# Asking for lam on another queue and taking its powers on GpSimd, in a linear-attention and gated feed-forward kernel

## The chip, the cores and the metric

The kernel runs on one core of a Trainium2 chip. The metric is device time in microseconds (us), the median of several executions: 204.59 us before the change, of three runs between 204.53 and 204.88. The profile is one execution of its own, with a span of 203.0 us. Engines are named PE (TensorE), ACT (ScalarE), DVE (VectorE), POOL (GpSimd) and SP (SyncE, which here only issues transfers).

## The reference, cut to what matters

Two stages follow each other: a linear attention with a decay per head, and a feed-forward layer whose gate is a cosine.

```python
# q, k, v: (4 batches, 8 heads, 768 positions, 64); lam: (8,), between 0.97 and 0.99
# attention, block by block of 64 positions:
intra = (q_b @ k_b.T * lam ** (i - j), lower triangle) @ v_b
inter = (q_b * lam ** (i + 1)) @ kv_state
out_b = intra + inter
kv_state = lam ** 64 * kv_state + (k_b * lam ** (63 - j)).T @ v_b
# feed-forward on x = attention output as (3072, 512):
h = x @ w_in            # 512 x 2048
result = (h * cos(h)) @ w_out   # 2048 x 512
```

Inputs and outputs are float32. Every decay in the formula is a power of lam with a position as exponent. A product of a power at the position of q and an inverse power at the position of k gives the same decay, and that is how the kernel uses it.

## The kernel before, in words

**Tiles.** The 3072 rows are cut into 24 blocks of 128 rows; one block holds all 8 heads. The feed-forward works on tiles of 2 or 4 blocks (`TILES`, L21). Each tile makes 16 slices of the hidden layer (`hidden`, L734, output `ps_h`), takes their cosine on ScalarE (`cosine`, L741), multiplies on VectorE (`gated`, L746), and multiplies with w_out (`project`, L779, output `ps_f`). Attention of the later blocks is worked in between.

**The spans.** The first four blocks are handled apart, as two spans of 256 rows (`add_span`, L584), so that the feed-forward can begin early. In a span each partition holds two neighbouring rows. The span's q and k come as float32 in loads of 512 KB on SyncE's queue (`add_span_load`, L274), in the order q, k of the first span, q, k of the second. `prep` (L597) multiplies them with `q_sp` and `k_sp`, powers of lam for two rows per partition; then they are turned on TensorE (L606), copied out by ScalarE (L609), and the scores, the state and the values follow. q and k of the first span and q of the second are scaled on VectorE, k of the second on GpSimd (`QK`, L32). The span's v comes through GpSimd's queue as bfloat16, unscaled, and is asked for only when the first q has landed.

**The other blocks.** `prepare` (L329) multiplies q with `q_scale` and v with `v_scale`, powers of lam for one row per partition and six blocks per batch.

**The powers, before.** They are made in the set-up, ahead of everything: lam is loaded to all 128 partitions (L187) as the first transfer on SyncE's queue, with 8 numbers per partition. ScalarE takes the logarithm (L215), VectorE multiplies with the positions (L217 and L222), and ScalarE takes four exponentials (L220 to L229), two of them with the sign turned. Logarithm, exponential and sine each need a table loaded on ScalarE, so there are three table loads (at L215, L220 and L231); the last is for the cosine. The positions are made by GpSimd's iota.

**What sets the order.** A planner in the kernel (`Planner`, L56) gives each task an engine, a duration and a priority, simulates the engines and writes the instructions out in the order of the simulated starts. `SETUP` (L61) says when each engine is done with the set-up. Between the planned tasks of TensorE `keep_awake` (L866) puts filler matmuls into `ps_idle`, as many as the plan has time for, until the main block of the first tile.

Of the kernel before, what the change touches and what calls it, by code (L numbers as in the profile page):

```python
# [10 lines left out]
F32 = mybir.dt.float32  # L11
BF16 = mybir.dt.bfloat16
AF = mybir.ActivationFunctionType
ALU = mybir.AluOpType
# [41 lines left out]
class Planner:  # L56


    LAT = {"PE": 0.2, "ACT": 0.06, "DVE": 0.08, "POOL": 0.1, "SP": 0.0, "DMA": 0.0, "SETUP": 0.0}

    SETUP = {"POOL": 3.7, "DVE": 5.6, "ACT": 7.3, "SP": 1.3, "DMA": 2.9}  # L61

    def __init__(self, bufs):
        self.tasks, self.bufs = [], bufs
# [6 lines left out]
    def order(self):  # L71
        free, done = dict(self.SETUP), []
        got = {tag: [] for tag in self.bufs}
# [70 lines left out]
def kernel(  # L144
# [10 lines left out]
    nc = tc.nc  # L155
    B, H, S, D = q.shape
    P = 128
    NB = S // P
# [9 lines left out]
    def where(n):  # L168

        if n < 2 * SPANS:  # L170
            return n // 2, n % 2
        g, c = divmod(n // 2, NB)
        return 2 * g + n % 2, c
# [3 lines left out]
    consts = ctx.enter_context(tc.tile_pool(name="consts", bufs=1))  # L177
# [5 lines left out]
    def bank(i, shape, dt, name):  # L183
        return psum.tile(shape, dt, tag=f"bank{i}", bufs=1, name=name)

    lam_bc = consts.tile([P, H], F32)
    nc.sync.dma_start(out=lam_bc, in_=bass.AP(tensor=lam.tensor, offset=lam.offset, ap=[[0, P], [1, H]]))  # L187
    pos = consts.tile([P, NB], F32)
    nc.gpsimd.iota(pos, pattern=[[P, NB]], base=-S // 2, channel_multiplier=1,
                   allow_small_or_imprecise_dtypes=True)  # L190
    ident = consts.tile([P, P], BF16)
    make_identity(nc, ident)
    pos_sp = consts.tile([P, 2], F32)
    nc.gpsimd.iota(pos_sp, pattern=[[1, 2]], base=-S // 2, channel_multiplier=2,
                   allow_small_or_imprecise_dtypes=True)
    mask_sp = consts.tile([P, 2, P], F32)
    nc.gpsimd.memset(mask_sp, 1.0)
    for i in range(2):
        m = mask_sp[i * D:(i + 1) * D].rearrange("u k (s t) -> u k s t", s=2)
        nc.gpsimd.affine_select(out=m, in_=m, compare_op=ALU.is_ge, fill=0.0,  # L200
                                base=0, pattern=[[-1, 2], [1, 2], [2, D]], channel_multiplier=-2)
    mask = consts.tile([P, D], F32)
    nc.gpsimd.memset(mask, 1.0)
    for i in range(2):
        m = mask[i * D:(i + 1) * D]
        nc.gpsimd.affine_select(out=m, in_=m, compare_op=ALU.is_ge, fill=0.0,
                                base=0, pattern=[[1, D]], channel_multiplier=-1)
# [3 lines left out]
    nc.vector.memset(blank, 0.0)  # L211
    kv_bd = consts.tile([P, 2, NP, P], BF16)
    nc.vector.memset(kv_bd, 0.0)
    lnl = consts.tile([P, H], F32)
    nc.scalar.activation(lnl, lam_bc, AF.Ln)  # L215
    expo_sp = consts.tile([P, H, 2], F32)
    nc.vector.tensor_mul(expo_sp, pos_sp.unsqueeze(1).to_broadcast([P, H, 2]),  # L217
                         lnl.unsqueeze(2).to_broadcast([P, H, 2]))
    q_sp = consts.tile([P, H, 2], F32)
    nc.scalar.activation(q_sp, expo_sp, AF.Exp)  # L220
    expo = consts.tile([P, NB, H], F32)
    nc.vector.tensor_mul(expo, pos.unsqueeze(2).to_broadcast([P, NB, H]),  # L222
                         lnl.unsqueeze(1).to_broadcast([P, NB, H]))
    k_sp = consts.tile([P, H, 2], F32)
    nc.scalar.activation(k_sp, expo_sp, AF.Exp, scale=-1.0)
    q_scale = consts.tile([P, NB, H], F32)
    nc.scalar.activation(q_scale, expo, AF.Exp)
    v_scale = consts.tile([P, NB, H], F32)
    nc.scalar.activation(v_scale, expo, AF.Exp, scale=-1.0)  # L229
    warm = consts.tile([P, 1], F32)  # L230
    nc.scalar.activation(warm, halfpi, AF.Sin)  # L231


    spare = consts.tile([P, 112], F32)
# [7 lines left out]
    pl = Planner({**BUFS, "q_f": BUFS["ld"], "k_f": BUFS["ld"], "v_f": BUFS["ld"]})  # L242
# [9 lines left out]
    def prio_attn(n, part):  # L252
        i = next(i for i in range(len(TILES)) if n < first[i + 1])
        return begins[i - 1] + unit[i - 1] * (n - n % 2 - first[i] + 2 * part) / TILES[i]

    load_t, issue_t = {}, {}
    last_issue = {}

    def dma(queue, us, issue_us, emit, prio, deps=(), get=None, ordered=True, lat=1.9):
        t = pl.add(queue, issue_us, list(deps) + [last_issue.get(queue) if ordered else None], emit, prio, get=get)  # L260
        if ordered:
            last_issue[queue] = t
        d = pl.add("DMA", us, [t], None, prio, lat=lat)
        d.issue = t
        return t, d
# [40 lines left out]
    w_t, pace = {}, []  # L306
# [15 lines left out]
    T, So, Vo, d_t, Uo, Uo_sp = ({} for _ in range(6))  # L322
    qkT_head, qk_head, v_head, v12 = {}, {}, {}, {}
# [5 lines left out]
    def prepare(pr):  # L329

        b, c = where(2 * pr)
        early = 2 * pr < TILES[0] + 2
        vec = {"DVE": nc.vector, "POOL": nc.gpsimd}
        us = {"DVE": 0.69, "POOL": 1.05}
        pa = lambda part: prio_attn(2 * pr, part)

        def new_qk():
            if ("qk", pr) not in live:
                live["qk", pr] = toks.tile([P, 2, H, 2, D], BF16, tag="qk", bufs=BUFS["qk"], name="qk")
            return live["qk", pr]  # L340

        def prep_q(_, s, e):
            vec[e].tensor_mul(new_qk()[:, 0, :, s], live.pop(("q_f", 2 * pr + s)),  # L343
                              q_scale[:, c, :].unsqueeze(2).to_broadcast([P, H, D]))

        def prep_k(_, s):
            (nc.scalar.copy if early else nc.gpsimd.tensor_copy)(new_qk()[:, 1, :, s], live.pop(("k_f", 2 * pr + s)))  # L347

        def prep_v(_, s, e):
            live["v_s", 2 * pr + s] = toks.tile([P, H, D], BF16, tag="v_s", bufs=BUFS["v_s"], name="v_s")  # L350
            vec[e].tensor_mul(live["v_s", 2 * pr + s], live.pop(("v_f", 2 * pr + s)),  # L351
                              v_scale[:, c, :].unsqueeze(2).to_broadcast([P, H, D]))

        a, k_ = [], []
        for s in range(2):
            n = 2 * pr + s
            eq = "DVE" if early and s == 0 else "POOL"
            ev = "DVE" if early and s == 1 else "POOL"
            a.append(pl.add(eq, us[eq], [load_t["q_f", n]] + a, partial(prep_q, s=s, e=eq), pa(-0.9), get=None if s else "qk"))
            k_.append(pl.add("ACT" if early else "POOL", 0.61, [load_t["k_f", n]] + ([] if early else [a[0]]), partial(prep_k, s=s), pa(-0.9)))  # L360
            d_t[n] = v_head[n] = pl.add(ev, us[ev], [load_t["v_f", n]], partial(prep_v, s=s, e=ev), pa(-0.85), get="v_s")
            for name, t in (("q_f", a[s]), ("k_f", k_[s]), ("v_f", d_t[n])):
                issue_t[name, n].frees = [t]

        def new_T():
            if ("qkT", pr) not in live:
                live["qkT", pr] = toks.tile([P, 2, H, P], BF16, tag="qkT", bufs=BUFS["qkT"], name="qkT")
            return live["qkT", pr]

        def transposes(t, i):  # L370
            live["t", pr, i] = bank(t.bank[0], [P, H, P], BF16, "ps_t")
            for h in range(H):
                nc.tensor.transpose(live["t", pr, i][:, h, :], live["qk", pr][:, i, h], ident)

        def transposes_out(_, i):
            nc.vector.tensor_copy(new_T()[:, i], live["t", pr, i])

        def transposes_dma(_, i):
            return nc.sync.dma_start_transpose(out=new_T()[:, i], in_=live["qk", pr][:, i].rearrange("t h s d -> t (h s d)"))

        for i, src in enumerate((a, k_)):
            get = None if i else "qkT"
            if 2 * pr >= DMA_FROM:
                head, T[pr, i] = dma("SP", 1.4, 1.3, partial(transposes_dma, i=i), 2 * pr + i - LAG + 1.5,
                                     src + ([qkT_head[pr]] if i else []), get=get, ordered=False)
                T[pr, i].lat = 1.2
                if i and 2 * pr + LAG < NBLK:
                    issue_t["q_f", 2 * pr + LAG].deps.append(head)
            else:
                t = pl.add("PE", MM(P, 8), src + ([T[pr, 0]] if i else []), partial(transposes, i=i), pa(-0.05 + 0.05 * i), banks=1)  # L390
                head = T[pr, i] = pl.add("DVE", 0.7, [t], partial(transposes_out, i=i), pa(0.0), get=get)
                t.bank_frees = [[head]]
            if i == 0:
                qkT_head[pr] = head
        qk_head[pr] = a[0]
# [76 lines left out]
    def add_stretch(pr):  # L472

        n0 = 2 * pr
        g, c = divmod(pr, NB)
        pa = lambda part: prio_attn(n0, part)
        tile_i, j0 = tile_of(n0)

# [343 lines left out]
    for at, name in enumerate(names):  # L822
        which, n = name[0], int(name[1:])
# [12 lines left out]
        else:  # L836
            kept.append(add_load(n, which + "_f", src[which], at, deps))

    idle = pl.add("SETUP", 0.0, [], None, -1e9, banks=1)
    for x in range(SPANS):  # L840
        add_span(x)
    add_span_state()
    for pr in range(SPANS, NBLK // 2):
        prepare(pr)
# [70 lines left out]
```

## Time and profile before

| | before |
|---|---|
| device time, median | 204.59 us |
| span of the profile | 203.0 us |
| busy: PE, DVE, ACT, POOL | 195.0, 116.7, 119.8, 64.5 us |
| PE busy on ps_h (L737) and on ps_f (L783) | 90.5, 88.3 us |
| lam: issue to landing | 3.0 us |
| the span's q and k (512 KB each): median issue to landing | 5.1 and 5.6 us |
| table loads in the set-up | 3 of 1.28 us |
| HBM traffic | 27.27 MB read, 6.29 MB written |

The page gives busy time by engine, then the span in 40 slices with a digit for the tenths that an engine was busy. The chain of waits is followed back from the last instruction, each step to what released it. A line of the timeline gives start, length, engine, line and operation, "output<-input" with the shapes, the count, and in brackets the idle time before it with what ended it; consecutive instructions of one kind are merged. The engine names with a q (SPq, POOLq) are the queues that issue transfers. A line of packets counts the pieces that the transfers moved in a stretch of time, and how many were below each size.

### The profile page before, as it was taken

How to read it: one execution, taken by the hardware profiler on the slowest of the kernel's cores; microseconds unless marked ns; L12 is line 12 of the kernel's file. 1: busy time of each engine (PE TensorE's matmuls, PEld its weight loads, DVE VectorE, ACT ScalarE, POOL GpSimd, SP SyncE). 2: the span in 40 equal slices, each digit the busy share in tenths (PEclk: the TensorE clock that was granted, in tenths of full speed). 3: DMA queues.
4: the chain of work that ended last, by engine and by line, in shares of the span. 5: the costliest groups of instructions: out<-in, count | busy, mean ns of one | idle time of the engine just before them, and what ended most of it. 6: DMA issues, size and time to landing. Idle time of an engine off the chain costs nothing.

```text
span 203.0 us, 5951 instructions
## 1 busy us (share of the span) xinstructions
PE 195.0 (96%) x2457; PEld 118.0 (58%) x2485; DVE 116.7 (57%) x229; ACT 119.8 (59%) x240; POOL 64.5 (32%) x85
## 2 busy tenths in 40 slices
PE   6999999999999999999999999999999999999993
PEld 2567444547747857767658676755446444444463
DVE  2887783257955967758458575835589544444001
ACT  5978871128838868565639666644887555354120
POOL 5794004066034262726455272543500000000000
PEclk9999999999999999999999999999999999999999
DMA  4999999989989999999999899979900010111112
GB/s 129 318 193 203 204 197 217 194 204 238 204 218 164 257 213 230 233 183 262 205 268 211 181 213 244 226 184 261 208 1 3 3 52 0 52 55 52 52 74 81
DMA packets 96906, 33.94 MB, mean 167 GB/s; under 512 B 84336, under 2 KB 93936, under 8 KB 96880
## 3 DMA queue, kind: packets, MB, share of 16 engines
q1 hardware_dynamic: 89376, 28.78, 64.8%
q0 software_dynamic: 7360, 4.72, 16.2%
q8 instruction: 19, 0.31, 0.6%
q10 hardware_dynamic: 144, 0.07, 0.1%
q14 instruction: 7, 0.06, 0.1%
HBM read 27.27 MB, written 6.29 MB: 165 GB/s over the span
## 4 chain that ended last, share of the span: by engine, by line
PE 84%; DMA 8%; SPq 2%; issue 2%; DVE 1%; POOL 1%; ACT 0%; POOLq 0%; ACTq 0%
PE ps_h L737 41%; PE ps_f L783 35%; DMA v_f<-in_v_dram 4%; DMA sp_f<-in_k_dram 3%; SPq L268 2%; DMA k_f<-in_k_dram 2%; PE ps_o L483 2%; PE ps_kv L433 2%; PE ps_o L515 2%; PE ps_s L421 1%; PE ps_o L643 1%; PE ps_kv L630 1%; POOL k_sp L598 1%; PE ps_x L483 0%; DVE v_s L351 0%
## 5 line engine op out<-in xcount | busy, mean ns | idle before, releaser
L749 DVE TENSOR_TENSOR g<-ps_h,cos 128x256 bf16<-128x256 f32 (+1 forms) x148 | 73.2, 503 | 42.9 <-ACT cos L743 42.0
L743 ACT ACTIVATE cos<-ps_h,halfpi 128x256 f32<-128x256 f32 (+1 forms) x148 | 75.6, 538 | 29.4 <-PE ps_h L737 28.6
L737 PE MATMUL ps_h<-xT,w_in_sb 128*128 128x256 bf16 (+1 forms) x586 | 90.5, 304 | 0.5 <-issue 0.3
L783 PE MATMUL ps_f<-w_out_sb,g 128*128 128x512 bf16 (+2 forms) x394 | 88.3, 362 | 2.0 <-issue 1.3
L737 PEld LDWEIGHTS <-w_in_sb 128*128 128x128 bf16 x592 | 57.1, 98 | 30.0 <-DVE xT L523 0.4
L783 PEld LDWEIGHTS <-g 128*128 128x128 bf16 x416 | 38.6, 98 | 36.3
L343 POOL TENSOR_TENSOR qk<-q_f,q_scale 128x512 bf16<-128x512 f32 x19 | 19.6, 1043 | 37.9 <-DMA q_f<-in_q_dram 33.6
L797 ACT COPY o_sb<-ps_f 128x512 f32<-128x512 f32 (+1 forms) x24 | 13.7, 572 | 30.3 <-PE ps_f L783 29.1
L351 POOL TENSOR_TENSOR v_s<-v_f,v_scale 128x512 bf16<-128x512 f32 x19 | 19.6, 1043 | 17.8 <-DMA v_f<-in_v_dram 14.4
L426 DVE TENSOR_TENSOR s_m<-ps_s,mask 128x512 bf16<-128x512 f32 x20 | 13.0, 684 | 3.6 <-PE ps_s L421 3.0
L347 POOL CAST qk<-k_f 128x512 bf16<-128x512 f32 x18 | 11.0, 611 | 7.0 <-DMA k_f<-in_k_dram 6.8
L523 ACT CAST xT<-ps_o 128x512 bf16<-128x512 f32 x11 | 6.0, 588 | 9.6 <-PE ps_o L515 6.3
L439 DVE TENSOR_TENSOR sum<-sum,ps_kv 128x512 f32<-128x512 f32 x15 | 10.2, 681 | 0.6
L444 ACT CAST S<-sum 128x512 bf16<-128x512 f32 x15 | 9.2, 617 | 0.9 <-DVE sum L439 0.8
L797 DVE COPY o_sb<-ps_f 128x256 f32<-128x256 f32 (+1 forms) x2 | 0.7, 358 | 11.2 <-PE ps_f L783 11.2
L875 PE MATMUL ps_idle<-blank 128*128 128x512 f32 (+2 forms) x8 | 5.4, 824 | 1.6 <-DVE blank L211 1.6
L483 PEld LDWEIGHTS <-v_s 64*64 64x64 bf16 x320 | 3.9, 107 | 4.1 <-issue 3.6
L622 DVE TENSOR_TENSOR s_m_sp<-ps_s,mask_sp 128x512 bf16<-128x512 f32 x8 | 5.1, 682 | 1.0 <-PE ps_s L617 1.0
L483 PE MATMUL ps_o<-s_m,v_s 64*64 64x64 bf16 x256 | 5.1, 196 | 0.1
L711 POOL CAST S<-sum 128x512 bf16<-128x512 f32 x1 | 0.6, 606 | 14.0 <-DVE sum L708 14.0
L500 DVE COPY spare<-ps_o 1x1 f32<-1x1 f32 x5 | 0.8, 156 | 7.3 <-PE ps_o L483 7.3
L515 PE MATMUL ps_o<-qkT,S 64*64 64x64 bf16 x304 | 4.8, 194 | 0.0
(74 smaller groups left out, 94.5 us busy)
## 6 DMA issues: line engine op xcount, KB each, us to landing
q_f<-in_q_dram SPq DMA_DIRECT2D x20, 256.0 KB, 3.8
k_f<-in_k_dram SPq DMA_DIRECT2D x20, 256.0 KB, 4.1
v_f<-in_v_dram SPq DMA_DIRECT2D x20, 256.0 KB, 4.7
out_dram<-o_sb SPq DMA_DIRECT2D x19, 256.0 KB, 2.6
w_out_sb<-in_moe_w_out_dram POOLq DMA_DIRECT2D x4, 512.0 KB, 12.6
out_dram<-o_sb SPq DMA_DIRECT2D x9, 128.0 KB, 3.4
sp_f<-in_q_dram SPq DMA_DIRECT2D x2, 512.0 KB, 5.1
sp_f<-in_k_dram SPq DMA_DIRECT2D x2, 512.0 KB, 5.6
```

Of the source, the lines that this page charges most:

```text
L343: vec[e].tensor_mul(new_qk()[:, 0, :, s], live.pop(("q_f", 2 * pr + s)), q_scale[:, c, :].unsqueeze(2).to_broadcast([P, H, D]))
L347: (nc.scalar.copy if early else nc.gpsimd.tensor_copy)(new_qk()[:, 1, :, s], live.pop(("k_f", 2 * pr + s)))
L351: vec[e].tensor_mul(live["v_s", 2 * pr + s], live.pop(("v_f", 2 * pr + s)), v_scale[:, c, :].unsqueeze(2).to_broadcast([P, H, D]))
L426: nc.vector.tensor_mul(t, live["s", pr][s], mask.unsqueeze(1).to_broadcast([P, H, D]))
L439: nc.vector.tensor_add(new, live["sum", pr, 0] if half else live["sum", pr - 1, 1], live["kv", pr][half])
L444: nc.scalar.copy(new_S(pr, half), live["sum", pr, half])
L483: yield lambda h=h: nc.tensor.matmul(o[halves[h % 2], h // 2], lhsT=live["v_s", n0 + s][m, h, :], rhs=live["s_m", n0 + s][m, h, :], start= ...
L737: nc.tensor.matmul(t[:, :n], lhsT=w_in_sb[:, kd, f * P:(f + 1) * P], rhs=live["xT", i][:, kd, at], start=(kd == 0), stop=(kd == KD - 1))
L743: nc.scalar.activation(c[:, :n], live["h", i, f, at.start][:, :n], AF.Sin, bias=halfpi)
L749: return nc.vector.tensor_mul(live["g", i][:, f, at], live.pop(("h", i, f, at.start))[:, :n], live.pop(("c", i, f, at.start))[:, :n])
L783: nc.tensor.matmul(live["f", i, j, piece][:, :width], lhsT=live["g", i][:, f, j * P:(j + 1) * P], rhs=w_out_sb[:, f, part], start=(f == 0) ...
L797: (nc.scalar.copy if eng == "ACT" else nc.vector.tensor_copy)(o[:, :width], live["f", i, j, piece][:, :width])
```

## The change

lam is asked for on ScalarE's queue, so that q stands first on SyncE's. The powers are no longer made by logarithm and exponential: GpSimd raises lam to the positions with its two-input power operation. For that the positions exist with both signs (four iotas instead of two). `scale_sp` (8 heads, two signs, two rows: 32 numbers per partition) is made at the end of GpSimd's set-up. `scale` (two signs, six blocks, 8 heads: 96 per partition) is a planned task `scales_t` of GpSimd, which stands after the issue of the third w_out piece; `prep_q` and `prep_v` of the other blocks depend on it. ScalarE keeps one table load, for the cosine. The numbers in `SETUP` are changed, which changes the sizes of a few fillers on TensorE: the first float32 run ends with 128 instead of 256 columns, one 512-column filler before the first scores is left out, and the one before the second span's k transposes has 512 instead of 320 columns. The other instructions keep their order on every engine.

```diff
-    SETUP = {"POOL": 3.7, "DVE": 5.6, "ACT": 7.3, "SP": 1.3, "DMA": 2.9}
+    SETUP = {"POOL": 4.0, "DVE": 4.5, "ACT": 2.6, "SP": 0.85, "DMA": 2.45}
...
-    nc.sync.dma_start(out=lam_bc, in_=bass.AP(tensor=lam.tensor, offset=lam.offset, ap=[[0, P], [1, H]]))
-    pos = consts.tile([P, NB], F32)
-    nc.gpsimd.iota(pos, pattern=[[P, NB]], base=-S // 2, channel_multiplier=1,
-                   allow_small_or_imprecise_dtypes=True)
+    nc.scalar.dma_start(out=lam_bc, in_=bass.AP(tensor=lam.tensor, offset=lam.offset, ap=[[0, P], [1, H]]))
+    pos = consts.tile([P, 2, NB], F32)
+    for i, sign in enumerate((1, -1)):
+        nc.gpsimd.iota(pos[:, i], pattern=[[sign * P, NB]], base=-sign * S // 2, channel_multiplier=sign,
+                       allow_small_or_imprecise_dtypes=True)
...
-    lnl = consts.tile([P, H], F32)
-    nc.scalar.activation(lnl, lam_bc, AF.Ln)
-    expo_sp = consts.tile([P, H, 2], F32)
-    nc.vector.tensor_mul(expo_sp, pos_sp.unsqueeze(1).to_broadcast([P, H, 2]),
-                         lnl.unsqueeze(2).to_broadcast([P, H, 2]))
-    q_sp = consts.tile([P, H, 2], F32)
-    nc.scalar.activation(q_sp, expo_sp, AF.Exp)
...
     warm = consts.tile([P, 1], F32)
     nc.scalar.activation(warm, halfpi, AF.Sin)
+
+    def power(out, p, lam_axis, pos_axis):
+        nc.gpsimd.tensor_tensor(out, lam_bc.unsqueeze(lam_axis).to_broadcast(list(out.shape)),
+                                p.unsqueeze(pos_axis).to_broadcast(list(out.shape)), op=ALU.pow)
...
+    scale_sp = consts.tile([P, H, 2, 2], F32)
+    power(scale_sp.rearrange("p h a s -> p h (a s)"), pos_sp.rearrange("p a s -> p (a s)"), 2, 1)
+    q_sp, k_sp = scale_sp[:, :, 0], scale_sp[:, :, 1]
+    scale = consts.tile([P, 2, NB, H], F32)
+    q_scale, v_scale = scale[:, 0], scale[:, 1]
...
+    def scales(_):
+        power(scale.rearrange("p a n h -> p (a n) h"), pos.rearrange("p a n -> p (a n)"), 1, 2)
+
+    scales_t = pl.add("POOL", 2.0, [], scales, -100.0)
...
-            a.append(pl.add(eq, us[eq], [load_t["q_f", n]] + a, partial(prep_q, s=s, e=eq), pa(-0.9), get=None if s else "qk"))
+            a.append(pl.add(eq, us[eq], [load_t["q_f", n], scales_t] + a, partial(prep_q, s=s, e=eq), pa(-0.9), get=None if s else "qk"))
...
+    scales_t.deps.append(w_t["out", 2].issue)
```

More of the change, by code (lines that the diff above doesn't have):

```diff
@@ L186 @@
     lam_bc = consts.tile([P, H], F32)
-    nc.sync.dma_start(out=lam_bc, in_=bass.AP(tensor=lam.tensor, offset=lam.offset, ap=[[0, P], [1, H]]))
-    pos = consts.tile([P, NB], F32)
-    nc.gpsimd.iota(pos, pattern=[[P, NB]], base=-S // 2, channel_multiplier=1,
-                   allow_small_or_imprecise_dtypes=True)
+    nc.scalar.dma_start(out=lam_bc, in_=bass.AP(tensor=lam.tensor, offset=lam.offset, ap=[[0, P], [1, H]]))
[3 more added lines that the diff above has]
+                       allow_small_or_imprecise_dtypes=True)
     ident = consts.tile([P, P], BF16)
     make_identity(nc, ident)
-    pos_sp = consts.tile([P, 2], F32)
-    nc.gpsimd.iota(pos_sp, pattern=[[1, 2]], base=-S // 2, channel_multiplier=2,
-                   allow_small_or_imprecise_dtypes=True)
+    pos_sp = consts.tile([P, 2, 2], F32)
+    for i, sign in enumerate((1, -1)):
+        nc.gpsimd.iota(pos_sp[:, i], pattern=[[sign, 2]], base=-sign * S // 2, channel_multiplier=2 * sign,
+                       allow_small_or_imprecise_dtypes=True)
     mask_sp = consts.tile([P, 2, P], F32)
@@ L213 @@
     nc.vector.memset(kv_bd, 0.0)
-    lnl = consts.tile([P, H], F32)
-    nc.scalar.activation(lnl, lam_bc, AF.Ln)
-    expo_sp = consts.tile([P, H, 2], F32)
-    nc.vector.tensor_mul(expo_sp, pos_sp.unsqueeze(1).to_broadcast([P, H, 2]),
-                         lnl.unsqueeze(2).to_broadcast([P, H, 2]))
-    q_sp = consts.tile([P, H, 2], F32)
[L220 to L229, printed above, removed]
     warm = consts.tile([P, 1], F32)
     nc.scalar.activation(warm, halfpi, AF.Sin)
+    def power(out, p, lam_axis, pos_axis):
[6 more added lines that the diff above has]
+    q_scale, v_scale = scale[:, 0], scale[:, 1]
     spare = consts.tile([P, 112], F32)
@@ L358, in prepare @@
             ev = "DVE" if early and s == 1 else "POOL"
-            a.append(pl.add(eq, us[eq], [load_t["q_f", n]] + a, partial(prep_q, s=s, e=eq), pa(-0.9), get=None if s else "qk"))
+            a.append(pl.add(eq, us[eq], [load_t["q_f", n], scales_t] + a, partial(prep_q, s=s, e=eq), pa(-0.9), get=None if s else "qk"))
             k_.append(pl.add("ACT" if early else "POOL", 0.61, [load_t["k_f", n]] + ([] if early else [a[0]]), partial(prep_k, s=s), pa(-0.9)))
-            d_t[n] = v_head[n] = pl.add(ev, us[ev], [load_t["v_f", n]], partial(prep_v, s=s, e=ev), pa(-0.85), get="v_s")
+            d_t[n] = v_head[n] = pl.add(ev, us[ev], [load_t["v_f", n], scales_t], partial(prep_v, s=s, e=ev), pa(-0.85), get="v_s")
             for name, t in (("q_f", a[s]), ("k_f", k_[s]), ("v_f", d_t[n])):
```

## The prediction

> **What bounds the kernel now.** I read the page first (engine shares and slices), then the stages, the chain of waits, and last the timeline and the transfers of the first microseconds, because the diff touches only work done there.
>
> From the page, the engine shares and the 40 slices:
>
> ```profile
> PE 195.0 (96%) x2457; PEld 118.0 (58%) x2485; DVE 116.7 (57%) x229; ACT 119.8 (59%) x240; POOL 64.5 (32%) x85
> PE   6999999999999999999999999999999999999993
> ```
>
> TensorE is full in all slices but the first and the last. The waits of TensorE from 15 us to the end add up to only 1.6 us (1.3 before the second product, 0.3 before the first). So the kernel is a start-up of about 11 us and then a solid block of matmuls; a change in the start-up is worth exactly what it moves the beginning of that block. The chain of waits says what sets the beginning (start us, length us, what):
>
> ```profile
> 0.81 0.40 SPq L187
> 1.26 0.42 SPq L268
> 1.73 0.58 SPq L268
> 2.35 1.54 SPq L268
> 3.93 5.95 DMA sp_f<-in_k_dram
> ...
> 10.06 1.05 POOL k_sp L598
> 11.16 0.40 PE ps_t L606 x4
> 11.55 0.55 PE ps_kv L630 x8
> ```
>
> The chain begins with the issue of lam (L187), goes through SyncE's queue and the fourth span load (the second k), then GpSimd's scaling of it, then TensorE, which never stops again. Busy TensorE before 11.16 us is filler (ps_idle). The other operations of that stage, from the timelines of ScalarE, VectorE and GpSimd (start us, length us):
>
> ```profile
> 3.79 0.21 ACT L215 ACTIVATE lnl<-lam_bc 128x8 f32<-128x8 f32 x1 [1.71 <-DMA lam_bc<-in_lam_dram]
> 4.02 1.28 ACT L220 ACT_TABLE_LOAD   x1
> 5.31 0.22 ACT L220 ACTIVATE q_sp<-expo_sp 128x16 f32<-128x16 f32 x1
> 5.56 1.29 DVE L598 TENSOR_TENSOR q_sp<-sp_f,q_sp 128x512 bf16<-128x512 f32 x2 [1.03 <-ACT q_sp L220]
> 6.99 1.29 DVE L598 TENSOR_TENSOR k_sp<-sp_f,k_sp 128x512 bf16<-128x512 f32 x2
> 8.42 1.29 DVE L598 TENSOR_TENSOR q_sp<-sp_f,q_sp 128x512 bf16<-128x512 f32 x2
> 5.63 1.96 POOL L268 DMA_DIRECT2D v_sp<-in_v_dram  x2 [1.97 <-DMA sp_f<-in_q_dram]
> 3.14 0.52 POOL L206 TENSOR_SCALAR_AFFINE_SELECT mask<-mask 64x64 f32<-64x64 f32 x2
> ```
>
> Two things end at nearly the same time. The first q was issued at 1.26 and took the shortest landing of the four, 4.1 us, so it was there at about 5.4; its scales (L220) were ready at 5.53. After that VectorE starts every 1.43 us (5.56, 6.99, 8.42), which is the pace at which 512 KB land (512 KB at the 348 GB/s seen here is 1.5 us), not the pace of its own 1.29 us. The start-up is paced by the load stream, and the scales only touch it at one point.
>
> What delays the stream? Packets moved by 2.4 us and by 3.4 us from the start:
>
> ```profile
> DMA packets 77, 0.01 MB, mean 2 GB/s; under 512 B 71, under 2 KB 77, under 8 KB 77
> DMA packets 321, 0.10 MB, mean 28 GB/s; under 512 B 142, under 2 KB 321, under 8 KB 321
> ```
>
> The small ones are lam: 128 reads of 32 B, one per partition. They stand ahead of q on the same queue, begin at about 1.85 us (1.0 us after their issue) and are gone at about 3.3 us. Only 6 packets of q have moved by 2.4, and full rate comes after 3.4. That is the most interesting line here: q loses lam's issue time and perhaps more.
>
> **What the Trainium skill says.** "DMA: Bandwidth & Descriptors", section on queues, rings and completion order: a queue's descriptors are taken in ring order on each engine, while an engine goes round-robin between rows, so lam on ScalarE's row need not stand before q. The packet counts agree with the first half; no run here shows the second yet. "ScalarE: Activation LUTs", section on what a table load costs: 1283 ns plus about 1380 ns of drain; the trace has the 1.28 us, and no drain (4.02 + 1.28 = 5.30, next operation 5.31). "GPSIMD Engine Reference", section on performance versus VectorE: two-input operations run at 2.6 cycles an element, data-dependent branching costs 12 more; the trace has 1.04 us for a 128x512 multiply, 2.03 ns or 2.4 cycles at the page's 1.2 GHz. No page prices a power operation.
>
> **The change, part by part.**
> *ScalarE.* Two table loads (2 x 1.28), the logarithm (0.21) and four exponentials (0.20 to 0.23) go, and the lam issue (0.40, as on SyncE) comes. The remaining Sine load now ends near 0.8 + 0.40 + 1.28 + 0.2 = 2.7 us instead of 7.4. Nobody waits for it: the first copy (L609) starts at 7.32 now only because ScalarE was loading until then, which holds the qT copies 0.4 us (their first transposes end at 6.92), but the path runs through k of the second span, far behind. Taken as zero.
>
> *VectorE.* Two small multiplies (0.18 and 0.20) go, in a 2 us idle stretch. Zero.
>
> *SyncE.* q is issued at 0.81 instead of 1.26: 0.45 us. All four span loads stand behind it in one queue, so if the stream keeps its shape each lands 0.45 earlier: q 4.95, k 6.5, second q 8.0, second k 9.43. That is the floor of the gain. If lam was the whole reason for the slow beginning, q runs at full rate from its first byte at 1.85: 1.85 + 1.5 + about 0.4 for completion = 3.8, a gain of 1.6 in the stream. That is the ceiling.
>
> *GpSimd.* Two more iotas (0.13 and 0.14, overlapped to about 0.1 each) move the end of its set-up from 3.66 to about 3.9. lam lands at 0.81 + 3.0 = 3.8 as before if ScalarE's row serves it like SyncE's. Then the power of 128x32. Low end: a multiply's 2.03 ns x 32 plus some 0.1 us = 0.2 us. High end: a power as logarithm, multiply and exponential, each priced at the page's 12 cycles, is 36 cycles or 30 ns an element, 0.96 us (an estimate); beyond that the same page, section on instruction dispatch, gives 6 us for the first call of a freshly loaded routine. I take the middle of the first two, 0.6: ready at 3.95 + 0.6 = 4.55. Behind it on GpSimd's queue stand the v issues (5.63 now, waiting for q) and w_in; VectorE waits for the power before its first q scaling. Ready at 4.55 against q at 3.8 to 4.95: it hides at the floor, and caps the gain at the ceiling: VectorE starts at 4.6 instead of 5.56, 0.96 us.
>
> The second power, 128x96, is three times the elements: 1.8 us at my price, 0.6 to 2.9 at the ends. In GpSimd's order it stands after the third w_out issue, at about 17.3 us, where GpSimd is idle for 14.0 us until 31.31; its first readers come at 32.71 (qk). Zero.
>
> *TensorE's fillers.* The order of real work is the same on all engines. One 512-column filler (0.38) goes before the first scores; that before the second span's k transposes grows from 320 to 512 float32 columns. The 320 took 0.76 with its weight loads from 10.18; 192 columns more, by the formula of `keep_awake` at L868 (2400 columns a us, shared by four passes), add 0.32. It starts after the second q's transposes, so it shifts with VectorE, ending about 0.1 later than the k scaling in the floor case (9.73 + 1.08 = 10.81 against 11.11 - 0.45 + 0.05 = 10.71). So the floor is worth 0.35 to 0.45.
>
> *What follows.* w_in, w_out and the q asked for at 29.63 all hang on span loads or on TensorE's own progress, so they shift along. The v load must come too: its first half lands at about 5.63 + 5.7 = 11.33 and is used at 11.48; its issue follows q and the power, so it moves by 0.45 to 1.0 as well.
>
> *Sum.* Between 0.4 (floor) and 0.96 (cap): I take 0.7, the middle, because the packet counts make lam guilty of some of the slow beginning, but the dips in q's own rate after 2.4 speak for a cold start that stays. 204.59 - 0.7 = 203.9.
>
> **The rivals.**
> 1. Only the issue is saved: 0.35 to 0.4, 204.2. For: the first q bytes also come 1.0 us after their issue, like lam's. Against: the small packets in front.
> 2. lam was the whole delay: 0.96 to 1.1, 203.6. Against: q's dips.
> 3. lam comes later on ScalarE's row, as its packets now alternate with those of q: at 5.0 the scales come at 5.6, as now, so 204.6. For: it needed 3.0 us even when it stood first.
> 4. The power is slow. Break-even is 5.53 - 3.95 = 1.6 us, 50 ns an element. At 75 ns it takes 2.4, is ready at 6.35, and holds both VectorE and the v issue by 0.8: 205.4; with a 6 us load, 209. For: nothing in the trace prices it. Against: it would need 90 cycles an element.
>
> **How the numbers follow.** Forecast 0.36, rivals 0.22, 0.17, 0.09 and 0.16. Faster by over 0.2% means under 204.18: forecast, rival 2, and somewhat over half of rival 1 (0.13): 0.66. The rest of rival 1 and most of rival 3 give same, 0.16; slower 0.18. The range 203.4 to 204.8 leaves out rival 4 and a thin tail below.
>
> **What would show it.** The q packets begin near 1.85 us; the first q scaling starts at 4.6 to 4.9; the power of 128x32 lasts 0.2 to 1.0 us and starts at about 3.95; second k lands near 9.2; its transposes start at about 10.5 instead of 11.16, and the first ps_h matmul at 14.5 instead of 15.18; the block after that keeps its length. Wrong if the power lasts over 1.6 us, if lam lands after 4.5, or if TensorE shows new waits after 15 us, above all for w_in.

## The result and the profile after

The change makes the kernel slower: 213.47 us (median of six runs, 212.80 to 214.86) against 204.74 us for the kernel before on the same chip (six runs, 204.53 to 205.07), a ratio of 1.0431 (1.0396 to 1.0465). The forecast was 203.9 us, with a range of 203.4 to 204.8.

The page of the kernel after, with the engine shares and three of the rows of 40 slices:

```profile
PE 197.2 (93%) x2456; PEld 119.0 (56%) x2484; DVE 119.5 (57%) x227; ACT 116.7 (55%) x233; POOL 86.7 (41%) x89
PE   7079999999999999999999999999999999999993
POOL 6999999124714445360736263553410000000000
PEclk9856999999999999999999999999999999999999
```

The span is 211.4 us, 8.4 more than before. TensorE is 2.2 us busier and 6.2 us more idle (211.4 - 197.2 = 14.2, against 203.0 - 195.0 = 8.0). The idle time sits in slices 2 and 3 of the row: TensorE is at 0 in the second slice and at 7 in the third, and its granted clock is 0.8, 0.5 and 0.6 in the second to fourth. From the fourth on TensorE's row is as before. GpSimd is full in slices 2 to 7.

The chain of waits says who holds the start (start us, length us, what):

```profile
0.80 3.62 DMA lam_bc<-in_lam_dram
4.57 5.46 POOL scale_sp L220
10.05 2.15 DVE q_sp L600 x2
12.20 2.92 DVE k_sp L600 x2
15.13 1.46 DVE q_sp L600
18.36 1.56 PE ps_idle L878 x2
```

Before, this stretch of the chain held the span's loads and nothing of the scales. Now it is lam, the first power, VectorE's scalings and a filler; the loads have left it. The timelines of GpSimd, VectorE and TensorE give the sizes:

```profile
4.57 5.46 POOL L220 TENSOR_TENSOR scale_sp<-lam_bc,pos_sp 128x32 f32<-128x32 f32 x1 [0.71 <-DMA lam_bc<-in_lam_dram]
10.05 2.15 DVE L600 TENSOR_TENSOR q_sp<-sp_f,scale_sp 128x512 bf16<-128x512 f32 x2 [7.89 <-POOL scale_sp L220]
12.12 3.00 DVE L600 TENSOR_TENSOR k_sp<-sp_f,scale_sp 128x512 bf16<-128x512 f32 x2
15.05 2.13 DVE L600 TENSOR_TENSOR q_sp<-sp_f,scale_sp 128x512 bf16<-128x512 f32 x2
10.80 0.61 PE L608 MATMUL ps_t<-ident,q_sp 128*128 128x128 bf16 x4 [5.04 <-DVE q_sp L600]
18.15 1.77 PE L878 MATMUL ps_idle<-blank 128*128 128x512 f32 x2
17.75 0.61 PE L608 MATMUL ps_t<-ident,q_sp 128*128 128x128 bf16 x4
19.76 0.39 PE L608 MATMUL ps_t<-ident,k_sp 128*128 128x128 bf16 x4
23.77 1.05 PE L739 MATMUL ps_h<-xT,w_in_sb 128*128 128x256 bf16 x8
```

The same of TensorE before:

```profile
9.94 0.40 PE L606 MATMUL ps_t<-ident,q_sp 128*128 128x128 bf16 x4
10.18 0.76 PE L875 MATMUL ps_idle<-blank 128*128 128x320 f32 x2
15.18 1.05 PE L737 MATMUL ps_h<-xT,w_in_sb 128*128 128x256 bf16 x8
```

The power of 32 numbers per partition takes 5.46 us, and VectorE waits 7.89 us for it. VectorE's six scalings then last 7.13 us instead of 4.15, because four of them take 1.53 to 1.55 us each and only two 0.68 and 0.69. TensorE waits 5.04 us before the first q transposes. The transposes of the second span's k (L608), the point where the solid block began at 11.16, come at 19.76. That is 8.60 later, in four terms:

| term | before | after | more |
|---|---|---|---|
| VectorE's first scaling starts | 5.56 | 10.05 | 4.49 |
| its six scalings, start to end | 4.15 | 7.13 | 2.98 |
| last scaling to last q transposes | 0.23 | 0.57 | 0.34 |
| from those to the k transposes | 1.22 | 2.01 | 0.79 |

In the last two terms TensorE is slow: the filler of 512 float32 columns takes 1.77 us in two passes, where 320 columns took 0.76; at full clock 512 columns take 1.08, as a trace below has it. The clock is recorded at 0.50 from 9.30 to 19.54 us. A run's mean clock says little of this, since a stretch without a record counts as 1.00: two of the six runs have a mean of 1.000 and took 213.68 and 213.85 us, no less than the three at 0.974 (212.80 to 213.25). From the first ps_h matmul on nothing has changed: 23.77 to the end of the span is 187.6 us, before 15.18 to the end is 187.8, and TensorE waits 1.3 and 0.3 us after it in both.

The packets moved by 2.4 and by 3.4 us, as they were shown of before, and of the second stretch the part of SyncE's queue:

```profile
DMA packets 32, 0.00 MB, mean 0 GB/s; under 512 B 32, under 2 KB 32, under 8 KB 32
DMA packets 251, 0.08 MB, mean 24 GB/s; under 512 B 99, under 2 KB 251, under 8 KB 251
q1 hardware_dynamic: 152, 0.08, 14.6%
```

q is issued 0.45 us earlier, yet SyncE's queue, which now carries q alone, has moved 152 packets by 3.4 us; before it had moved 321, of which 142 were lam's. lam lands at 4.42 instead of 3.79. Both halves of the change miss what they were for.

### The profile page after: what moved, and what is told of

Same layout as the page of the kernel before. It is cut to its first block, busy times and chain, and to the rows that moved or that the text cites. A ratio compares the mean times of both kernels' runs of the same rounds, so it can differ in the third digit from the quotient of the medians.

```text
span 211.4 us, 5942 instructions
## 1 busy us (share of the span) xinstructions
PE 197.2 (93%) x2456; PEld 119.0 (56%) x2484; DVE 119.5 (57%) x227; ACT 116.7 (55%) x233; POOL 86.7 (41%) x89
## 4 chain that ended last, share of the span: by engine, by line
PE 89%; DVE 3%; POOL 3%; DMA 2%; issue 1%; ACT 0%; ACTq 0%; POOLq 0%
PE ps_h L739 40%; PE ps_f L785 39%; POOL scale_sp L220 3%; DMA lam_bc<-in_lam_dram 2%; DVE q_sp L600 2%; PE ps_o L485 2%; PE ps_s L423 1%; PE ps_o L517 1%; PE ps_kv L435 1%; DVE k_sp L600 1%; PE ps_t L608 1%; PE ps_idle L878 1%; PE ps_s L619 1%; PE ps_o L645 1%; PE ps_kv L632 1%
## 5 line engine op out<-in xcount | busy, mean ns | idle before, releaser
L345 POOL TENSOR_TENSOR qk<-q_f,scale 128x512 bf16<-128x512 f32 x19 | 19.6, 1043 | 34.4 <-DMA q_f<-in_q_dram 22.1
L353 POOL TENSOR_TENSOR v_s<-v_f,scale 128x512 bf16<-128x512 f32 x19 | 19.8, 1042 | 16.6 <-DMA v_f<-in_v_dram 12.6
L220 POOL TENSOR_TENSOR scale<-lam_bc,pos 128x96 f32<-128x96 f32 x1 | 15.7, 15732 | 0.0
L600 DVE TENSOR_TENSOR q_sp<-sp_f,scale_sp 128x512 bf16<-128x512 f32 x4 | 4.3, 1110 | 7.9 <-POOL scale_sp L220 7.9
L611 ACT COPY qT_sp<-ps_t 128x512 bf16<-128x512 bf16 x4 | 2.3, 586 | 11.0 <-PE ps_t L608 11.0
L608 PE MATMUL ps_t<-ident,q_sp 128*128 128x128 bf16 x16 | 2.4, 308 | 5.7 <-DVE q_sp L600 5.7
L878 PE MATMUL ps_idle<-blank 128*128 128x512 f32 (+1 forms) x8 | 6.0, 903 | 1.6 <-DVE blank L213 1.6
L799 DVE COPY o_sb<-ps_f 128x256 f32<-128x256 f32 (+1 forms) x2 | 0.7, 358 | 11.2 <-PE ps_f L785 11.2
```

What stands on the lines that cost most here:

```text
L220: nc.gpsimd.tensor_tensor(out, lam_bc.unsqueeze(lam_axis).to_broadcast(list(out.shape)), p.unsqueeze(pos_axis).to_broadcast(list(out.shape ...
L600: vec[e].tensor_mul(place(L[name], hp), live[name + "_f", "sp", x][:, cut[hp]], (q_sp if name == "q" else k_sp)[:, cut[hp]].unsqueeze(3).t ...
L799: (nc.scalar.copy if eng == "ACT" else nc.vector.tensor_copy)(o[:, :width], live["f", i, j, piece][:, :width])
```

## The experiments

Ratios are to the kernel before on the same chip, with 95% intervals.

### What a power costs

Before the change nothing in the trace priced GpSimd's power. `pow_sizes` is the kernel before with four more operations on GpSimd after the third w_out issue; nobody reads their results. The arguments are partitions, place, heads, exponents and operation.

```diff
+        spare_power(P, 0, 8, 4, ALU.mult)
+        spare_power(P, 0, 8, 1, ALU.pow)
+        spare_power(P, 1, 8, 4, ALU.pow)
+        spare_power(1, 2, 8, 4, ALU.pow)
```

> The kernel before, with four extra GpSimd operations whose results nobody reads, in the 14 us in which GpSimd is idle: a multiply of 128x32, a power of 128x8, a power of 128x32, a power of one partition x32. Theory (the power costs about 165 ns for each element of a partition, 5.46 for 32 and 15.73 for 96): multiply about 0.2 us, powers 1.6 and 5.5 us. Rival (the first call of a routine is what costs): the 128x8 takes 5 us or more, the others under 1. One partition: about 5.5 us if all lanes run side by side, about 0.4 to 0.7[...]. Time as before, 204.7, since all of it is in an idle stretch.

The four in order, from the trace:

```profile
18.69 0.32 POOL L259 TENSOR_TENSOR spare_p<-lam_bc,pos 128x32 f32<-128x32 f32 x1
19.09 1.68 POOL L259 TENSOR_TENSOR spare_p<-lam_bc,pos 128x8 f32<-128x8 f32 x1
20.74 5.41 POOL L259 TENSOR_TENSOR spare_p<-lam_bc,pos 128x32 f32<-128x32 f32 x1
26.13 5.40 POOL L259 TENSOR_TENSOR spare_p<-lam_bc,pos 1x32 f32<-1x32 f32 x1
```

The multiply takes 0.32 us, the power of 8 numbers per partition 1.68, of 32 numbers 5.41, and of 32 numbers on a single partition 5.40. With 15.73 us for the 96 numbers of the changed kernel, a line through the three sizes is about 160 ns a number and 0.3 to 0.4 us for the instruction. The number of partitions makes no difference here (1 or 128), and the first power carries no extra: no load of a routine shows, only a long price per number. The time of this kernel, 206.27 us in its single run, is no measure of that: its second k landed at 11.32 us instead of 9.88, well before the powers began at 19.09.

### Each half alone

`queue_only` is the kernel before with nothing but the new place of lam:

```diff
-    nc.sync.dma_start(out=lam_bc, ...)
+    nc.scalar.dma_start(out=lam_bc, ...)
```

> The kernel before, with only lam moved to ScalarE's queue and q first on SyncE's; logarithm and exponential stay. Prediction's theory: q and all span loads land 0.45 us earlier, a gain. New theory (both rows serve slower while they start together, as the trace after shows lam at 4.42 and full rate only after 4.4): lam lands about 0.6 later, the scales at 6.1 instead of 5.53, the second k at 10.4 instead of 9.88, so 205.2 to 205.5. If the load stream's lateness was chance: 204.6 to 205.3 by the scales alone.

It took 205.84 us, 1.0039 (1.0017 to 1.0061): slightly slower. VectorE's first scaling and GpSimd's of the second k, both 0.7 to 0.8 later than before (5.56 and 10.06):

```profile
6.29 1.29 DVE L598 TENSOR_TENSOR q_sp<-sp_f,q_sp 128x512 bf16<-128x512 f32 x2 [1.03 <-ACT q_sp L220]
10.83 2.04 POOL L598 TENSOR_TENSOR k_sp<-sp_f,k_sp 128x512 bf16<-128x512 f32 x2 [0.96 <-DMA sp_f<-in_k_dram]
```

The first ps_h follows at 15.95 instead of 15.18. So in this trace half of the change makes the load stream 0.77 us later, not 0.45 earlier; over all traces, below, the delay is nearer 0.5.

`pow_only` is the changed kernel with lam back on SyncE's queue, ahead of q:

```diff
-    nc.scalar.dma_start(out=lam_bc, ...)
+    nc.sync.dma_start(out=lam_bc, ...)
```

> The changed kernel with lam back as the first transfer on SyncE's queue; the powers on GpSimd stay. Theory (the first power sets the path): lam lands at 3.8 instead of 4.42, the power runs 3.95 to 9.4 instead of 4.57 to 10.03, VectorE's six scalings follow at once, 0.6 us faster than the change: 212.9. Rival (the queue change is a large part of the loss): 211 or less.

213.3 us, 1.0401 (1.0382 to 1.0421). The power runs from 3.95 to 9.41, so VectorE starts 0.6 earlier than in the changed kernel, as expected; but one of its scalings then takes 2.40 us and the filler 2.02 at the low clock, and the k transposes gain 0.4 (19.34). The power half alone is nearly the whole loss.

### A short power

`after_8_powers` is the changed kernel with a first power of 8 numbers per partition in place of 32: one per head, spread over both rows and both signs, and exponents counted from 64. The scales of the two spans are thereby not the reference's.

```diff
-        nc.gpsimd.iota(pos_sp[:, i], pattern=[[sign, 2]], base=-sign * S // 2, channel_multiplier=2 * sign,
+        nc.gpsimd.iota(pos_sp[:, i], pattern=[[sign, 2]], base=64, channel_multiplier=2 * sign,
...
-    power(scale_sp.rearrange("p h a s -> p h (a s)"), pos_sp.rearrange("p a s -> p (a s)"), 2, 1)
-    q_sp, k_sp = scale_sp[:, :, 0], scale_sp[:, :, 1]
+    power(scale_sp[:, :, 0, 0:1], pos_sp[:, 0, 0:1], 2, 1)
+    q_sp = k_sp = scale_sp[:, :, 0, 0:1].to_broadcast([P, H, 2])
```

> The changed kernel with only 8 of the 32 first powers made and spread over both rows, both signs (so the scales of the spans are wrong numbers; their exponents start at 64 so that values stay small). Everything else as in the change. Theory (the length of the first power sets the loss, 0.32 + 0.16 a number): it lasts 1.7 us, VectorE starts at 6.3 as in the run with only the queue changed, no cold clock, no slow scalings, 205.8 to 206.1. Rival (a power costs much whatever its size, or other parts of the change cost too): 208 or more.

206.08 us, 1.0045 (1.0024 to 1.0066). GpSimd's two powers and TensorE's filler of 512 columns, from an execution of 207.47 us, 1.4 over the median, whose second k landed late (11.54):

```profile
4.70 1.68 POOL L220 TENSOR_TENSOR scale_sp<-lam_bc,pos_sp 128x8 f32<-128x8 f32 x1 [0.83 <-DMA lam_bc<-in_lam_dram]
18.91 15.72 POOL L220 TENSOR_TENSOR scale<-lam_bc,pos 128x96 f32<-128x96 f32 x1
11.89 1.08 PE L878 MATMUL ps_idle<-blank 128*128 128x512 f32 x2
```

With 3.78 us less of power the ratio falls from 1.0431 to 1.0045, some 7.9 us of 204.9. The slow scalings are gone (all six at 0.68 to 0.69), no fall of the clock is recorded in the start-up, and the filler of 512 columns takes 1.08 us. The ratio that is left is about that of the queue alone (1.0039). The second power is still there with its 15.72 us, and the time leaves no room for it: it is hidden.

### Why the first wait costs almost double

Two consequences of the wait stood in the trace: a low clock and slow scalings. `after_awake` is the changed kernel with five more 512-column fillers in front of the first transposes, so that TensorE is busy while it waits.

```diff
+            if now < 2.0:
+                keep_awake(4.4, 8.0)
```

> The changed kernel with five more 512-column filler matmuls at the start, so that TensorE works while the power runs and its clock is not lowered to a half. Theory (the clock is a side cost: 0.3 us behind VectorE's scalings and 0.8 in the filler before the second k): 1.0 to 1.2 us faster than the change, 212.3, and the scalings on VectorE still take 1.5 us each because GpSimd works beside them. Rival (the slow scalings come from the low clock too): 4 us faster, 209.5.

The expected gain did not come: 214.41 us, 1.0468 (1.0437 to 1.0499), no faster than the changed kernel. Five stretches of it (start:end and length in us; busy time of PE, PEld, DVE, ACT and POOL, each with its count; then the granted clock, the DMA share and GB/s):

```profile
12.00:14.00 2.00, 0.79 (x8) 0.46 (x9) 2.00 (x3) 0.59 (x1) 2.00 (x4) 1.00 1.25 114
14.00:16.00 2.00, 1.14 (x17) 0.61 (x18) 2.00 (x2) 0.65 (x2) 2.00 (x2) 0.61 1.74 175
16.00:20.00 4.00, 3.73 (x42) 1.98 (x39) 3.69 (x6) 1.70 (x3) 4.00 (x7) 0.50 1.42 185
11.05:14.46 3.41, 1.71 (x15) 0.71 (x13) 3.41 (x3) 1.38 (x3) 3.41 (x5) 1.00 0.98 91
14.46:21.28 6.82, 5.71 (x57) 3.50 (x58) 5.23 (x7) 2.68 (x5) 6.82 (x9) 0.50 1.45 180
```

The clock holds until 14.46 us and is at half until 21.28 (the last two stretches). The fillers moved the low clock from a thin stretch into a fuller one. They also show that the slow scalings are not the clock's doing: VectorE has the same 2.15, 3.00 and 2.13 us.

The Trainium skill, "TensorE: Matmul & The Clock Gate", the part on the clock gate, gives half speed after an idle window of about 3.4 us. The changed kernel agrees: TensorE is idle from 5.8 to 10.8 us, and the clock falls at 9.30. In `after_awake` no gap was over 0.86 us and the clock fell all the same; the page's idle window does not cover that, and the measurement stands. What the falls share is a stretch of little work. In all 13 traces the clock's records last whole multiples of 3.41 us, leaving out the one cut off by a trace's end. In the five falls of the start-ups the 3.41 us before had TensorE busy for 0, 0, 0.20, 0.49 (`pool_mul`, below) and 0.50 of the time (here, 1.71 us), while the least busy such stretch without a fall had 0.56 (`queue_only`, 4.75 to 8.16 us). These are observations; a limit was not measured.

`after_k1_dve` is the changed kernel with the second span's k scaled on VectorE too, so that GpSimd multiplies nothing while VectorE does.

```diff
-QK = [{...}, {"q": ("DVE", "DVE"), "k": ("POOL", "POOL")}]
+QK = [{...}, {"q": ("DVE", "DVE"), "k": ("DVE", "DVE")}]
```

> The changed kernel with k of the second span scaled on VectorE instead of GpSimd. Theory (a scaling on VectorE that reads two SBUF tiles waits while GpSimd reads SBUF): the scalings that overlapped GpSimd's two k scalings return from 1.5 to 0.69 us; if issuing v and w_in on GpSimd also holds VectorE, the ones beside those stay at 1.5. Rival (cold clock or the strided scale tile): all keep 1.5 us. Time about 213 to 215, as two scalings more stand in VectorE's queue behind the score copies; the lengths tell, not the time.

212.99 us, 1.0365 (1.0318 to 1.0412). VectorE's scalings, two per line, and GpSimd beside them:

```profile
10.17 1.29 DVE L600 TENSOR_TENSOR q_sp<-sp_f,scale_sp 128x512 bf16<-128x512 f32 x2 [8.01 <-POOL scale_sp L220]
11.38 1.29 DVE L600 TENSOR_TENSOR k_sp<-sp_f,scale_sp 128x512 bf16<-128x512 f32 x2
12.59 1.29 DVE L600 TENSOR_TENSOR q_sp<-sp_f,scale_sp 128x512 bf16<-128x512 f32 x2
10.11 2.01 POOL L270 DMA_DIRECT2D v_sp<-in_v_dram  x2
```

All six are back at 0.69 us, although GpSimd issues v and w_in beside them. So it was GpSimd's two multiplies that slowed VectorE. The time gained little, as the two extra scalings now stand behind score work on VectorE (17.11) and the k transposes come at 18.95.

To see the same without any power, `pool_mul` adds three multiplies to the set-up of the kernel before, their product unread; `pool_copy` has `tensor_copy(unread, blank)` in their place.

```diff
+    unread = consts.tile([P, 4 * P], F32)
+    for _ in range(3):
+        nc.gpsimd.tensor_mul(unread, blank, blank)
```

> The kernel before with three multiplies of two 128x512 tiles added at the end of GpSimd's set-up, their product unread; nothing else is changed. Theory (a GpSimd instruction that reads SBUF holds VectorE's two-input scalings): the multiplies take GpSimd from 3.7 to about 6.9 us, and the scalings that VectorE starts at 5.56 and 6.2 take 1.1 to 1.6 us each in place of 0.69; the last two, from 8.4 on, keep 0.69. Rival (the scalings of the changed kernel were slow for another reason): all six stay at 0.69. Both: v is asked for about 1.2 us later, the time rises by about 1 us.

> The same with three copies of one 128x512 tile in place of the multiplies. If any GpSimd instruction that reads SBUF holds VectorE, the scalings that overlap them take over 1.1 us as well; if it needs two inputs on GpSimd, all six stay at 0.69 us.

`pool_mul`, 206.17 us in its one run; GpSimd's multiplies and VectorE's scalings:

```profile
3.75 3.60 POOL L216 TENSOR_TENSOR unread<-blank 128x512 f32<-128x512 f32 x3
5.66 2.24 DVE L601 TENSOR_TENSOR q_sp<-sp_f,q_sp 128x512 bf16<-128x512 f32 x2 [0.60 <-ACT k_sp L228]
```

Its four scalings of q as a group (shortest, median, longest in ns):

```profile
L601 DVE TENSOR_TENSOR q_sp<-sp_f,q_sp x4: 677/737/1521, 5.7 to 9.6; 128x512 bf16<-128x512 f32 x4
```

Of the two scalings that start before the multiplies end at 7.35, the one at 5.66 takes 0.80 us and the one at 6.38, beside the last multiply, 1.52; that multiply takes 1.36 in place of 1.04. All later scalings take 0.68. A 16-number multiply of VectorE that met the first GpSimd multiply took 0.74 us in place of 0.18. The Trainium skill, "SBUF — State Buffer", section on who interferes with whom, says it: a VectorE instruction with two SBUF inputs contends with a GpSimd instruction that reads SBUF, as an exclusive lock for the whole instruction. The trace agrees, with 1.52 against 0.69. In `pool_copy` (205.15 us, one run) all six scalings stay at 0.69, but the copies were shorter than I had assumed and ended at 5.69, 0.05 after the first scaling began; that run therefore says nothing on large copies. The small multiply that met them took 0.27.

### Why q did not come earlier

Two kernels change the kernel before, with its logarithm and exponentials, so that lam is one row of 32 bytes. A matmul with ones spreads it over the partitions into PSUM. In `lam_row_sp` the row is asked for first on SyncE's queue; `lam_row_act` asks on ScalarE's, q first.

```diff
-    nc.sync.dma_start(out=lam_bc, in_=bass.AP(... ap=[[0, P], [1, H]]))
-    nc.scalar.activation(lnl, lam_bc, AF.Ln)
+    nc.sync.dma_start(out=lam_row, in_=bass.AP(... ap=[[0, 1], [1, H]]))
...
+    nc.tensor.matmul(idle_ps[:, :320], ...)
+    nc.tensor.matmul(lam_ps, lhsT=ones, rhs=lam_row, start=True, stop=True)
+    nc.scalar.activation(lnl, lam_ps, AF.Ln)
...
-    now = 1.6
+    now = 2.9
```

> The kernel before (logarithm and exponential) with lam loaded as one row into one partition, first on SyncE's queue, and spread to all partitions by a small matmul with ones between the fillers; the logarithm reads it from PSUM. Theory of the prediction (the 128 packets of lam hold up q): q reaches full rate near 2.9 us instead of 3.5, the second k lands at 9.3 instead of 9.9, the scales are ready near 4.7, 204.0 to 204.2 against 204.7. Rival (a cold start of the transfers, whatever goes first): second k at 9.9, 204.7.

> The same with the one-row load of lam on ScalarE's queue and q first on SyncE's. Theory of the prediction (without lam's packets the issue time of 0.45 us is won as well): second k at 8.9 to 9.4, 203.6 to 204.2. Rival (starting two queues together, or q first, slows the beginning): second k at 10.4 as in the change, 205.2.

Packets of SyncE's queue other than the small ones of lam, the start of GpSimd's scaling of the second k, and the landing of the second k in every trace that has lam in this form and place (all in us):

| kernel | lam | by 3.4 us | by 4.2 us | by 5.0 us | k scaling | k landed, all such traces |
|---|---|---|---|---|---|---|
| before | 128 reads, SyncE, first | 179 | 683 | 1240 | 10.06 | 9.88, 9.97, 10.10, 10.11, 11.32 |
| lam_row_sp | 1 row, SyncE, first | 194 | 715 | 1256 | 10.06 | 9.89 |
| queue_only | 128 reads, ScalarE | 140 | 400 | 875 | 10.83 | 10.47, 10.58, 10.58, 10.66, 11.54 |
| lam_row_act | 1 row, ScalarE | 487 | 1035 | 1585 | 9.48 | 9.24, 9.31 |

The last column shows the scatter: 11.32 (`pow_sizes`) and 11.54 (`after_8_powers`) are about 1 us late in their rows for no reason known here, so two single traces compare poorly, and `before` has the earliest landing of its row. First two rows: without the crowd of small packets ahead of it q is hardly faster. It has 194 packets by 3.4 us, against 97 to 179 in the five traces of the first row, and the second k lands at 9.89 against a median of 10.10. So the crowd cost some 0.2 us at most where it stood; the rest of the slow beginning is q's own. Last row: with q issued first and no crowd beside it the 0.45 us does arrive; the scaling of the second k starts 0.58 earlier than before. Third row: the same crowd on a second queue costs 1.35 us between 9.48 and 10.83, and against the first row the stream is 0.5 us later by the medians (10.58 and 10.10). Between 3.4 and 4.2 us, until the last of lam's packets moved, q gets 260 packets (234 to 274 in the five traces) where it gets 504 (460 to 504) when lam stands in front. That a transfer engine takes turns between queues, as the prediction quoted, fits this; how much of a turn one small packet takes was not measured.

`lam_row_sp` took 205.10 us, 0.9992 (0.9969 to 1.0016), no different; `lam_row_act` 204.84, 0.9978 (0.9956 to 0.9999), at the edge of being faster than the kernel before. Its k transposes came at 11.20 all the same, since its 960 columns of filler, put behind the matmul that waits for lam, hold the first transposes until 6.91. So I shortened them:

```diff
-    now = 2.9
+    now = 4.2
...
```

> The kernel with lam as one row on ScalarE's queue, with 576 columns of filler after the spreading of lam in place of 960. Theory (the gain of the stream was stopped by fillers in front of the first transposes): the first transposes move from 6.9 to about 6.1 us, the second k, scaled by about 10.5, sets the k transposes again at 10.6 (11.16 in the kernel before), and the time is 0.5 under the kernel before, a ratio of about 0.997. Rival (score copies and second q set the k transposes anyway): k transposes at 11.0 or later, ratio 0.998 to 1.000.

204.83 us, 0.9987 (0.9967 to 1.0006): no gain to be seen. TensorE in `lam_row_act`, then in the short one:

```profile
3.54 3.57 PE L857 MATMUL ps_idle<-blank 128*128 128x512 f32 x4
8.67 0.39 PE L588 MATMUL ps_t<-ident,k_sp 128*128 128x128 bf16 x4
11.20 0.39 PE L588 MATMUL ps_t<-ident,k_sp 128*128 128x128 bf16 x4
```

```profile
3.54 2.40 PE L857 MATMUL ps_idle<-blank 128*128 128x512 f32 x4
6.14 0.61 PE L588 MATMUL ps_t<-ident,q_sp 128*128 128x128 bf16 x4 [0.20 <-DVE q_sp L580]
8.67 0.63 PE L588 MATMUL ps_t<-ident,k_sp 128*128 128x128 bf16 x4
11.52 0.39 PE L588 MATMUL ps_t<-ident,k_sp 128*128 128x128 bf16 x4
```

The first transposes do start at 6.14 instead of 6.91. But a group of four transposes takes 0.63 us up to the one at 8.67, where the trace with the longer fillers has 0.39 to 0.42 from 7.8 us on. By 8.67 the lead is gone, and the k transposes come 0.32 later. The clock row shows 1.00 in both. But the traces' records of the clock begin only at 7.81 and at 9.60 us, and the row counts 1.00 where there is none. In all 13 traces the first record lies between 4.5 and 11.2 us, and in the 11 in which TensorE works just then it stands where TensorE turns fast; before it a bfloat16 filler of 512 columns takes 0.63 us, as it does under the recorded half clock, and after it 0.38. So TensorE begins at about half its speed, and the row doesn't show it. When that ends varies: with the same first fillers it ended at 4.75, 4.86, 5.83, 6.34 and 7.47 us in five traces. One trace each can't show that the shorter fillers caused the later end here.

## Why the prediction was wrong, point by point

**The step that failed.** "I take the middle of the first two, 0.6: ready at 3.95 + 0.6 = 4.55." The first power takes 5.46 us, ready at 10.03. The 0.2 to 0.96 us were built from a multiply's price and a guess of three plain operations; 5.46 us less 0.3 for the instruction is about 160 ns for each of the 32 numbers, about 190 cycles at the 1.2 GHz that the prediction used, where I argued that 90 would be too many. Rival 4 had the mechanism. Its outer value was close in length (6 us), but by luck: it came from a load of the routine, and in `pow_sizes` the first power takes 1.68 us, which leaves no room for one.

**Rival 4's sum, too low.** It gave 209 for 6 us. The wait alone is 4.49 us of VectorE's start, and as much again came from what it met: GpSimd's two multiplies, which before began after VectorE was done, now fell among its scalings (2.98), and TensorE, idle for 5.04 us, worked at half its clock (0.34 and 0.79). I had treated a delay as a shift of everything behind it. Between engines that share something, a delay of one against the other is not a shift.

**The second step that failed.** "If the stream keeps its shape each lands 0.45 earlier ... That is the floor of the gain." The stream came 0.77 later in `queue_only`, about 0.5 by the medians of the traces. By this, even a power of no length would not have made the change faster (no run has one): the queue half by itself is at 1.0039, on the other side of my forecast. Rival 3 had this, with lam at 5.0 us (it landed at 4.42) and the packets taking turns; it left the loads untouched, and they came later too.

**"The packet counts make lam guilty of some of the slow beginning."** Guilty of little at most: in `lam_row_sp` the second k lands at 9.89, against a median of 10.10 with the small packets in front. The other reading, a cold start of q's own, holds for the rest.

**What held.** ScalarE's lost table loads and VectorE's two multiplies were worth nothing: ScalarE is done at 2.75 us (I had 2.7), and no one waited for it. GpSimd's set-up ended at 3.86 (3.9). The second power is hidden, though 15.7 us long and not 1.8: it ends at 36.9, and GpSimd then waits another 2.98 us for VectorE's sum before its next work. With a margin of 3 us left, an idle stretch of 14 us was less safe than I wrote. The work keeps its order, and the block after the start-up keeps its length: its start moved by 8.60 us and the time by 8.73.

**Signs named beforehand.** The power lasts over 1.6 us: yes. lam after 4.5: almost, 4.42, and 4.50 to 4.56 in the four other traces with these reads on ScalarE's queue. New waits of TensorE in the block after the start-up: none.

## What to carry to other kernels

Where no row of the profile prices an operation, an upper bound put together from other operations' prices is still a guess. If the chain of waits can't bear a much higher price, measure the operation first, in three sizes, in an idle stretch. A transfer of many tiny packets that is moved to a second queue need not step aside: here it slowed the large one, and a single row did not, so cut it to a single row before moving it. A delay in a start-up can cost more than its own length: look at which two engines it will newly put side by side, and at how long it lets TensorE rest. And compare several traces before a difference of half a microsecond in a load is given a cause.

## What the runs showed of the hardware that was not expected

- GpSimd's power costs about 160 ns for each number of a partition and 0.3 to 0.4 us for the instruction: 1.68, 5.41 to 5.46 and 15.73 us for 8, 32 and 96. One partition costs as much as 128 (5.40 and 5.41).
- A two-input VectorE operation took 1.52 us instead of 0.69 beside a GpSimd multiply. In the changed kernel VectorE's scalings slow from 10.66 us on, but GpSimd's multiplies are recorded only from 13.48, behind issues of v and w_in; without them the slowness is gone. Why it begins before their recorded start stays open.
- 128 packets of 32 bytes on a second queue made a stream of four 512 KB loads about 0.5 us later than the same packets ahead of it on its own queue (medians of five traces each, 10.58 and 10.10); with a single row of 32 bytes there it came about 0.8 earlier (9.24 and 9.31).
- The granted clock fell to half with no gap over 0.86 us in `after_awake` (for 6.8 us) and none over 0.92 in `pool_mul` (for 3.4 us); in both TensorE was busy for about half of the 3.41 us before the fall.
- TensorE begins each trace slow (0.63 us for a bfloat16 filler of 512 columns, then 0.38) without a record of the clock; in 11 of 13 it is seen to turn fast, between 4.5 and 11.2 us.
